# Attention values of the last 64 keys in quarters of the array, for two slots at once, and the copy of x ahead of the split

## The chip, the cores and the metric

The kernel runs on one core of a Trainium2 chip. The engines named here are TensorE (PE, with its weight loads as PEld), VectorE (DVE), ScalarE (ACT), GpSimd (POOL) and SyncE (SP, which here only issues DMAs). The metric is the device time of one execution in microseconds (us). Three runs of the kernel before gave a median of 1435.09 us, from 1433.96 to 1436.72.

## What is computed

Attention over 8 batches, 8 heads, 576 positions and a head size of 64, in which each row keeps only its 32 largest scores; then a feed-forward block with a sigmoid-gated unit. All is float32.

```python
scores = scale * np.matmul(q, k.transpose(0, 1, 3, 2))      # 576 x 576 for each batch and head
kth = np.partition(scores, -32, axis=-1)[..., -32:-31]
scores = np.where(scores >= kth, scores, -1e9)
attn = softmax(scores)
x = np.matmul(attn, v)            # (8,8,576,64), then heads side by side: 4608 rows x 512
h = x @ w_in                      # 512 x 2048
g = h / (1 + exp(-1.702 * h))
out = g @ w_out                   # 2048 x 512
```

## The kernel before

**Slots.** The work of the attention is cut into 144 slots, 18 for each batch. A slot holds 128 query rows of two heads (a pair `hp`, four pairs in a batch), so 2 x 576 scores for each of its rows. A batch has 576 = 4 x 128 + 64 rows; the last 64 rows of two pairs share one slot, so two slots of each batch are such end slots (`t == NF`), in which the two pairs take 64 columns each.

**What a slot goes through.** PE makes the scores in 64x64 quarters of its array (`scores`, L312): the contraction is over a head's 64 dimensions, one head in the upper and one in the lower half of the array's rows, and each head's scores go to banks of their own. ACT copies them out of PSUM with the scale (`copy_scores`, L324). DVE makes pairwise maxima and minima of the two halves of each row (`pair_up`, L334, two TENSOR_TENSOR), and then finds the 32 largest in four rounds of MAX8 with MATCH_REPLACE8 between them (`topk`, L348 and L352). POOL makes two small bounds (`bounds`, L366 and L367), ACT masks (L379) and takes exponentials with their sums (L387). DVE inverts the sums (`invert`, L395 and L397, the tile `rden`), POOL multiplies the probabilities by it (`normalize`, L410, two instructions), and ACT splits each float32 into its two 16-bit halves (`split`, L446). SP writes these to DRAM (L448) and reads them back transposed (`turn_by_dma`, L454) into the tile `pt`, in which keys lie on the partitions. `pt` has nine blocks of 128 keys: four whole blocks of the one head, one block made of the last 64 keys of both heads (the one head on partitions 0 to 63, the other on 64 to 127), and four whole blocks of the other head.

**Values.** `values_at` (L504) multiplies `pt` with the values `v`: for each slot five products for each head, 128 keys deep and 64 columns wide in the array, so that the two heads run side by side. The fifth product uses the tile `tail` (v_e in the profile): the 64 last keys of head j lie in the half of the partitions that belongs to head j in `pt`, and the other half of the partitions is zero, so that the product runs over all 128 partitions and drops the other head's keys. Tails are loaded by `load_v` (L218, two DMAs) into four tiles that stay. ACT copies the result out of PSUM (`x_of`, L527, L530) into `xs`, the input of the feed-forward block.

**Feed-forward.** Four slots complete a block of 128 rows of x. `hidden` (L570) makes 4 of 16 pieces of h for a block, in one bank `ph`; ACT takes the tanh (L586) and copies h (L589); POOL forms the gate (`gate`, L598 and L599) and four sums (`combine`, L623 to L626) for a product by a scheme with seven instead of eight block products; PE projects (`project`, L677). When a block is done ACT copies the two banks (L695), and POOL adds the seven products up (`merge_all`, five TENSOR_TENSOR, L702) before the output leaves.

**Order.** The order of the instructions of every engine is written out by hand. From slot 13 on it is the order of `two_slots(n)` (L1018), called for every second n. One call holds, for PE: two `hidden`, scores of n+2, two projections, the values of slots n-3 and n-2 (`held`), scores of n+3. DVE finds the largest of slot n and of n+1 (`find`, L956): 14 instructions of `topk` with `pair_up` of the next slot after the eighth (i == 7), and `invert` of the slot before after instruction `at`, which is 8. POOL: merge_all, combine, normalize(n-1), gate, bounds(n), combine, normalize(n), gate, bounds(n+1). ACT: split(n-1), copy_scores(n+2), mask and exponentials of n, tanh and h, split(n), x_of, copy_scores(n+3), mask and exponentials of n+1, tanh and h. While `filling` (up to n = 19) x_of stands right behind the values instead.

**PSUM.** Eight banks: two score tiles of two banks each, two for the projection, and two in the pool `ps_t`, which hold in turn the two `ph` and the one `o` (values) of each call. A tile of the pool waits until the tile two before it has been read.

Of the kernel before, what the change touches and what calls it, by code (L numbers as in the profile page):

```python
# [11 lines left out]
F32 = mybir.dt.float32  # L12
# [6 lines left out]
P = 128  # L19
# [11 lines left out]
def kernel(  # L31
# [27 lines left out]
    nc = tc.nc  # L59

    B, H, S, D = q.shape
# [3 lines left out]
    NF = S // P  # L65
    FULL = NF * P
    TAIL = S - FULL
# [9 lines left out]
    MAIN = (0, NF + 1)  # L77
# [29 lines left out]
    xs = const.tile([P, PLACES, CC, P], F32, name="xT")  # L107
# [5 lines left out]
    ps_t = pool("ps_t", 2, space=PSUM)  # L113
# [52 lines left out]
    qT, kT, vv = {}, {}, {}  # L166
# [41 lines left out]
    def load_v(b, hp):  # L208
        main = vals.tile([P, 2, NF, D], F32, name="v_l")
        nc.sync.dma_start(  # L210
            main[:].rearrange("p j t d -> p j (t d)"),
            v[b, 2 * hp : 2 * hp + 2, 0:FULL, :].rearrange("j (p t) d -> p j (t d)", t=NF),
        )


        tail = v_ends[(b * NP + hp) % len(v_ends)]
        for j in range(2):
            nc.sync.dma_start(tail[j * TAIL : (j + 1) * TAIL, j, :], v[b, 2 * hp + j, FULL:S, :])  # L218
        vv[b, hp] = main, tail

    def prepare_main(name, b, hp):
# [68 lines left out]
    second_part = []  # L290


    slots = []
    for b in range(B):

        full = [(b, t, (hp, hp)) for t in range(NF) for hp in range(NP)]
        ends = [(b, NF, (hp, hp + 1)) for hp in range(0, NP, 2)]
# [2 lines left out]
    PER = N // B  # L300
    st = [{} for _ in slots]

    def scores(n):
        b, t, hps = slots[n]
        ps = [ps_s.tile([P, 2, 512], F32, name="s_ps") for _ in range(2)]
        quadrants = (0, 0), (1, 1), (0, 1), (1, 0)
        of = lambda p: slice(t * P + p * TAIL, t * P + (p + 1) * TAIL) if t < NF else slice(FULL, S)
        parts = [(i, p, slice(p * TAIL, (p + 1) * TAIL), of(p)) for i, p in quadrants]
        for c in range(2):
            for i, p, rows, cols in parts:  # L310
                on = slice(i * D, (i + 1) * D)
                nc.tensor.matmul(  # L312
                    ps[i][rows, c, 0:HALF],
                    lhsT=qT[b, hps[p]][on, cols],
                    rhs=kT[b, hps[p]][on, FIRST[i] + c * HALF : FIRST[i] + (c + 1) * HALF],
                )
        st[n]["ps"] = ps
# [10 lines left out]
    def pair_up(n):  # L328

        sc = st[n]["sc"]  # L330
        a, b = sc[:, :, 0:HALF], sc[:, :, HALF:S]
        ranked[n] = rank.tile([P, 2, 2, HALF], F32, name="ranked")
        for c, op in enumerate((ALU.max, ALU.min)):
            nc.vector.tensor_tensor(out=ranked[n][:, :, c, :], in0=a, in1=b, op=op)  # L334
# [34 lines left out]
    def exponentials(n, between=lambda: None):  # L369

        mask(n)
        between()
        exps(n)
# [18 lines left out]
    def invert(n):  # L392

        some = small.tile([P, 2], F32, name="some", tag="sums")
        nc.vector.tensor_scalar_add(some[:], st[n]["den"][:], 1e-9)  # L395
        rden = st[n]["rden"] = small.tile([P, 2], F32, name="rden", tag="inverse")
        nc.vector.reciprocal(rden[:], some[:])  # L397
# [44 lines left out]
    def split(n):  # L442

        pr, sc = st[n]["pr"], st[n]["sc"]
        halves = sc[:].rearrange("p i k -> p (i k)").bitcast(U16).rearrange("p (h k) -> p h k", h=2)
        nc.scalar.copy(out=halves, in_=pr[:].bitcast(U16).rearrange("p (k h) -> p h k", h=2))  # L446
        rows = st[n]["rows"] = apart.tile([P, 2, 2 * S], U16, name="rows")
        nc.sync.dma_start(rows[:], halves)  # L448
# [10 lines left out]
    def place_of(b, t):  # L459

        name = (b, t) if t < NF else b // 2
        if name not in places:
            places[name] = free.pop(0)
        return places[name]
# [39 lines left out]
    def values_at(m, o):  # L504

        b, t, hps = slots[m]
        pt = st[m]["pt"]
        for p in range(2 if t == NF else 1):
            cols = slice(p * TAIL, (p + 1) * TAIL) if t == NF else slice(0, P)
            main, tail = vv[b, hps[p]]  # L510
            for c in range(NF + 1):
                for j in range(2):
                    nc.tensor.matmul(  # L513
                        o[j * D : (j + 1) * D, cols],
                        lhsT=main[:, j, c, :] if c < NF else tail[:, j, :],
                        rhs=pt[:, MAIN[j] + c if c < NF else NF, cols],
                        start=(c == 0),
                        stop=(c == NF),
                    )
        st[m].clear()  # L520

    def x_of(held, o):

        b, t, hps = slots[held[0]]
        x = xs[:, place_of(b, t), :, :]
        if t < NF:
            nc.scalar.copy(out=x[:, hps[0] : hps[0] + 2, :], in_=o[:, 0:2, :])  # L527
        else:
            parts = o[:, 0:2, :].rearrange("p s (h r) -> p (s h) r", h=2)
            nc.scalar.copy(out=x[:, :, b % 2 * TAIL : (b % 2 + 1) * TAIL], in_=parts)  # L530
        for m in held:
            finish_x(m)

    def finish_x(m):

        b, t, hps = slots[m]
        if hps[-1] < NP - 1:
            return
        if t == NF:
            if b % 2:  # L540
                first = [(b - 1 + i) * S + FULL for i in range(2)]
                ready.append(Block(places.pop(b // 2), [out[x : x + TAIL, :] for x in first]))
            return
        lines = out[b * S : b * S + FULL, :].rearrange("(p t) c -> p t c", t=NF)[:, t, :]
        ready.append(Block(places.pop((b, t)), [lines[i * TAIL : (i + 1) * TAIL, :] for i in range(2)]))
# [189 lines left out]
    def at(n, fn, *args):  # L735
        later.setdefault(n, []).append((fn, args))
# [36 lines left out]
    def finish_one():  # L773
        unfinished.pop(0)()
# [179 lines left out]
    live = lambda m: 0 <= m < N  # L954

    def find(m, at):  # L956

        for i, op in enumerate(topk(m) if live(m) else [lambda: None] * 14):
            op()
            if i == 7 and live(m) and live(m + 1):  # L960
                pair_up(m + 1)
            if i == at and live(m - 1):
                invert(m - 1)
            if i > 1 and len(unfinished) > (2 if m == SETTLED + 1 else 0):
                finish_one()

    def project_one():
        if may_project(0):
            project(True)
# [48 lines left out]
    def two_slots(n):  # L1018

        begin, prepare_some = dues(n)  # L1020
        aside = n < N
        filling = n < STEADY + 8
        if live(n - 1):
            exponentials(n - 1)
        if n == STEADY or n > STEADY + 4:
            prepare_some()
        hidden(ps_t)
        hidden(ps_t)
        tanh(aside)
        if live(n + 2):  # L1030
            scores(n + 2)
        project_one()
        merge_all()
        combine()
        project_one()
        find(n, 8)
        if live(n - 1):
            normalize(n - 1)
            split(n - 1)
        gate()  # L1040
        begin(0)
        if live(n - 1):
            turn_by_dma(n - 1)
        while turns:
            turns.pop(0)()
        if live(n + 2):
            copy_scores(n + 2)
        if live(n):
            bounds(n)
            mask(n)  # L1050
        combine()
        sum_weights(4)
        if live(n):
            exps(n)
        tanh(aside)
        prepare_some()
        held = [m for m in (n - 3, n - 2) if live(m)]
        o = ps_t.tile([P, 4, P], F32, name="o", tag="tp") if held else None
        ends = [(b, hp, o[:, 2 + i, :]) for i, (b, hp) in enumerate(second_part)]
        second_part.clear()  # L1060
        for what in ends:
            turn_qk_ends(*what)
        for i, m in enumerate(held):
            values_at(m, o[:, i, :])
        if filling and held:
            x_of(held, o)
        for what in ends:
            copy_qk_ends(*what)
        if filling:
            begin(1)  # L1070
        if live(n + 3):
            scores(n + 3)
        leave_all()
        find(n + 1, 8)
        if live(n):
            normalize(n)
            split(n)
        if held and not filling:
            x_of(held, o)
        if not filling:  # L1080
            begin(1)
        if live(n):
            turn_by_dma(n)
        gate()
        if live(n + 3):
            copy_scores(n + 3)
        if live(n + 1):
            bounds(n + 1)
        sum_weights(4)
# [51 lines left out]
```

## Time and profile before

| what | value |
|---|---|
| median of 3 runs | 1435.09 us |
| the profiled execution's own time | 1434.99 us |
| its span | 1433.1 us |
| mean granted TensorE clock | 0.982 |
| busy: PE, PEld | 1374.1 us (96%), 1233.0 us (86%) |
| busy: DVE | 1345.1 us (94%) |
| busy: ACT, POOL | 1165.1 us (81%), 959.3 us (67%) |
| from the values' first matmul at 291.6 us to that at 1343.5 us (58 calls of `two_slots`) | 1051.9 us; PE busy 1048.6, DVE busy 1044.4 |
| DMA share in that stretch | 0.76, granted clock 1.00 |

The chain of work that ended last gives shares of the span to the instruction that was being waited for, so it names the engine that sets the time. The timeline lists instructions by start and length in us; an instruction's successor on its engine can start before its end is recorded. "idle before, releaser" says what ended an engine's wait. A float32 matmul stands in the profile as two MATMUL instructions.

### The profile page before, as it was taken

To read this page: it belongs to the slowest core of one execution; us is meant where nothing else is said; L and a number is where in the kernel's file an instruction comes from. 1 tells how busy PE (TensorE), PEld (TensorE's weight loads), DVE (VectorE), ACT (ScalarE), POOL (GpSimd) and SP (SyncE) were. 2 spreads that over 40 slices of the span, in tenths; PEclk is the share of its full clock that TensorE was granted. 3 is DMA by queue.
4 is the path that set the end of the run, shared out by engine and by line. 5 is a ranking of instruction groups with operands and counts; after the bars stand their busy time and mean duration, and the time that the engine had idled before them with its cause. 6 is when DMAs were issued, how large, how long until landed. Compare 5 with 4: busy or idle time off the path is not lost.

```text
span 1433.1 us, 45827 instructions
## 1 busy us (share of the span) xinstructions
PE 1374.1 (96%) x18164; PEld 1233.0 (86%) x18164; DVE 1345.1 (94%) x3526; ACT 1165.1 (81%) x1895; POOL 959.3 (67%) x1602
## 2 busy tenths in 40 slices
PE   6779797899999999999999999999999999999997
PEld 5667476799999999999999999999899999999997
DVE  7999998999999999999999999999999999999712
ACT  6998777888888888888888888888888888888811
POOL 4787694677766777777777777777666677777710
PEclk8899899999999999999999999999999999999999
DMA  7452465878687788778787887887887786655520
GB/s 223 141 152 72 126 155 151 195 189 195 169 203 184 192 192 201 202 182 187 190 208 180 187 196 182 198 190 189 185 208 189 182 205 175 175 141 141 141 58 16
DMA packets 535991, 245.47 MB, mean 171 GB/s; under 512 B 458976, under 2 KB 514273, under 8 KB 535777
## 3 DMA queue, kind: packets, MB, share of 16 engines
q1 hardware_dynamic: 535344, 242.25, 68.0%
q8 instruction: 142, 2.33, 0.7%
q14 instruction: 73, 0.59, 0.1%
q10 hardware_dynamic: 432, 0.30, 0.1%
HBM read 45.09 MB, written 103.42 MB: 104 GB/s over the span
## 4 chain that ended last, share of the span: by engine, by line
PE 81%; DVE 9%; ACT 4%; POOL 2%; DMA 2%; issue 1%; SPq 0%; POOLq 0%; ACTq 0%; DVEq 0%
PE ph L570 32%; PE po L677 28%; PE o L513 10%; PE s_ps L312 9%; DVE top L348 4%; DVE ranked L352 2%; DVE left L352 1%; DVE ranked L334 1%; DMA pt<-rows 1%; ACT pr L387 1%; DMA qk_t<-qk_rows 1%; PE tp L424 1%; POOL pr L410 1%; ACT sc L379 0%; PE po L570 0%
## 5 line engine op out<-in xcount | busy, mean ns | idle before, releaser
L348 DVE MAX8 top<-ranked 128x8 f32<-128x288 f32 (+1 forms) x1080 | 598.8, 596 | 0.0
L570 PEld LDWEIGHTS ph<-xT,win 128*128 128x128 f32 x4384 | 495.2, 192 | 32.1 <-ACT sc L446 14.9
L570 PE MATMUL ph<-xT,win 128*128 128x128 f32 x4384 | 509.2, 277 | 2.5 <-ACT xT L527 2.5
L352 DVE MATCH_REPLACE8 ranked<-top,ranked 128x288 f32<-128x288 f32 (+1 forms) x810 | 433.5, 543 | 0.0
L410 POOL TENSOR_SCALAR pr<-pr,rden 128x576 f32<-128x576 f32 x268 | 197.7, 749 | 319.2 <-DVE rden L397 196.1
L446 ACT COPY sc<-pr 128x2304 uint16<-128x2304 uint16 x134 | 283.5, 2116 | 130.9 <-POOL pr L410 130.5
L334 DVE TENSOR_TENSOR ranked<-sc 128x576 f32<-128x576 f32 x270 | 218.9, 852 | 3.2 <-ACT sc L324 3.2
L387 ACT ACTIVATE pr<-sc,low 128x576 f32<-128x576 f32 x288 | 220.3, 773 | 0.0
L379 ACT ACTIVATE sc<-sc,cut 128x576 f32<-128x576 f32 x288 | 207.8, 778 | 4.6 <-POOL cut L366 4.6
L677 PE MATMUL po<-raws,h 128*64 128x128 f32 x2048 | 198.8, 273 | 0.0
L677 PE MATMUL po<-wout,h 128*64 128x128 f32 x2048 | 198.8, 273 | 0.0
L324 ACT ACTIVATE sc<-s_ps 128x576 f32<-128x576 f32 x288 | 171.7, 650 | 21.7 <-PE s_ps L312 10.8
L312 PE MATMUL s_ps<-qk_t 64*64 64x288 f32 x2304 | 177.1, 420 | 3.8 <-ACT sc L324 2.2
L599 POOL TENSOR_TENSOR th<-th,h 128x512 f32<-128x512 f32 x130 | 166.5, 1281 | 10.8
L677 PE MATMUL po<-wout,th 128*64 128x128 f32 x2176 | 168.6, 276 | 0.0
L513 PE MATMUL o<-pt,v_l 128*64 128x128 f32 (+1 forms) x2400 | 146.8, 267 | 8.1 <-DMA pt<-rows 6.7
L677 PEld LDWEIGHTS po<-wout,th 128*64 128x64 f32 x2176 | 124.3, 137 | 28.2 <-issue 20.6
L513 PEld LDWEIGHTS o<-pt,v_l 128*64 128x64 f32 x2400 | 128.5, 140 | 9.9 <-DMA pt<-rows 7.3
L677 PEld LDWEIGHTS po<-raws,h 128*64 128x64 f32 x2048 | 129.5, 137 | 0.0
L677 PEld LDWEIGHTS po<-wout,h 128*64 128x64 f32 x2048 | 129.4, 137 | 0.0
L702 POOL TENSOR_TENSOR raws<-raws 128x128 f32<-128x128 f32 (+1 forms) x165 | 93.5, 575 | 47.3 <-ACT raws L695 39.5
L312 PEld LDWEIGHTS s_ps<-qk_t 64*64 64x64 f32 x2304 | 76.1, 134 | 52.9 <-issue 14.6
(106 smaller groups left out, 1725.0 us busy)
## 6 DMA issues: line engine op xcount, KB each, us to landing
rows<-sc SPq DMA_DIRECT2D x134, 576.0 KB, 3.5
qk_rows<-halves SPq DMA_DIRECT2D x48, 256.0 KB, 3.0
out_dram<-raws SPq DMA_DIRECT2D x136, 64.0 KB, 2.3
raws<-in_moe_w_in_dram SPq DMA_DIRECT2D x16, 512.0 KB, 4.4
v_l<-in_v_dram SPq DMA_DIRECT2D x32, 256.0 KB, 3.9
raws<-in_moe_w_out_dram SPq DMA_DIRECT2D x16, 512.0 KB, 3.5
qk_l<-in_q_dram SPq DMA_DIRECT2D x60, 128.0 KB, 3.4
qk_l<-in_k_dram SPq DMA_DIRECT2D x58, 128.0 KB, 3.5
```

Source lines behind the costliest of these rows:

```text
L312: nc.tensor.matmul(ps[i][rows, c, 0:HALF], lhsT=qT[b, hps[p]][on, cols], rhs=kT[b, hps[p]][on, FIRST[i] + c * HALF : FIRST[i] + (c + 1) * ...
L324: nc.scalar.mul(out=to, in_=ps[i][:, :, 0:HALF], mul=SCALE)
L334: nc.vector.tensor_tensor(out=ranked[n][:, :, c, :], in0=a, in1=b, op=op)
L348: nc.vector.max(top[:, i, 8 * r : 8 * r + 8], of(r, i))
L352: nc.vector.match_replace(to, top[:, i, 8 * r : 8 * r + 8], of(r, i), LOWEST)
L379: nc.scalar.activation(sc[:, i, :], sc[:, i, :], AF.Prelu, bias=cut[:, i : i + 1], alpha=HUGE)
L387: nc.scalar.activation(pr[:, i * S : (i + 1) * S], sc[:, i, :], AF.Exp, bias=low[:, i : i + 1], accum_out=den[:, i : i + 1],)
L410: nc.gpsimd.tensor_scalar(pr[:, i, :], pr[:, i, :], st[n]["rden"][:, i : i + 1], 1.0, op0=ALU.mult, op1=ALU.mult)
L446: nc.scalar.copy(out=halves, in_=pr[:].bitcast(U16).rearrange("p (k h) -> p h k", h=2))
L513: nc.tensor.matmul(o[j * D : (j + 1) * D, cols], lhsT=main[:, j, c, :] if c < NF else tail[:, j, :], rhs=pt[:, MAIN[j] + c if c < NF else ...
L570: nc.tensor.matmul(ph[:, i * P : (i + 1) * P], lhsT=win[:, c, f * P : (f + 1) * P], rhs=xs[:, x.place, c, :], start=(c == 0), stop=(c == C ...
L677: nc.tensor.matmul(both_banks[y * TAIL : (y + 1) * TAIL, bank, r * P : (r + 1) * P], lhsT=a[:, i, :], rhs=weight(w, fs[i])[:, y * P : (y + ...
```

## The change

1. `load_v`: from the second batch on, each of the two DMAs of a tail brings both heads' last 64 keys (64 x 2 x 64 elements instead of 64 x 64), so both halves of the partitions hold both heads.
2. `scores`: in the slots with odd number of these batches the heads stand in opposite order (`crossed`): the head in the lower half of the array comes first in the scores and so in `pt`.
3. `values_of_two` takes the place of `values_at` for these batches: first the 16 products over whole blocks of both slots, as before; then, for the last 64 keys, four products of 64 x 64 in the four quarters of the array, two for each slot. The slot's heads in opposite order make the four quarters different ones. Each slot has a bank of its own: `o` becomes two tiles of `ps_t`.
4. `x_of`: one copy for each slot (128 x 128) instead of one for both (128 x 256), and, after the filling, in front of `split(n)` instead of behind it.
5. `find(n, 10)` and `find(n + 1, 10)` instead of 8: `invert` of the slot before stands two DVE instructions later, behind the second MAX8 and the first MATCH_REPLACE8 of the third round.

```diff
         for j in range(2):
-            nc.sync.dma_start(tail[j * TAIL : (j + 1) * TAIL, j, :], v[b, 2 * hp + j, FULL:S, :])
+            on, heads = slice(j * TAIL, (j + 1) * TAIL), slice(j, j + 1) if b == 0 else slice(0, 2)
+            src = v[b, 2 * hp + heads.start : 2 * hp + heads.stop, FULL:S, :]
+            nc.sync.dma_start(tail[on, heads, :], src.rearrange("j p d -> p j d"))
...
+    crossed = lambda n: n % 2 == 1 and slots[n][0] > 0
...
             for i, p, rows, cols in parts:
-                on = slice(i * D, (i + 1) * D)
+                j = 1 - i if crossed(n) else i
+                on = slice(j * D, (j + 1) * D)
...
+    def values_of_two(held, o):
+        order = []
+        for s, m in enumerate(held):
+            b, t, hps = slots[m]
+            pt = st[m]["pt"]
+            for p in range(2 if t == NF else 1):
+                cols = slice(p * TAIL, (p + 1) * TAIL) if t == NF else slice(0, P)
+                main, tail = vv[b, hps[p]]
+                at = lambda i: 1 - i if crossed(m) else i
+                for c in range(NF):
+                    for i in range(2):
+                        order.append((0, s, p, i, at(i), cols, main[:, at(i), c, :], pt[:, MAIN[i] + c, cols]))
+                for i in range(2):
+                    on = slice(i * TAIL, (i + 1) * TAIL)
+                    order.append((1, p, s, i, at(i), cols, tail[on, at(i), :], pt[on, NF, cols]))
+            st[m].clear()
+        bank_of = lambda x: (x[2] if x[0] else x[1], x[4])
+        order.sort(key=lambda x: x[:4] if x[0] else (0,))
+        for k, (ends, p, s, i, j, cols, lhsT, rhs) in enumerate(order):
+            if not ends:
+                p, s = s, p
+            nc.tensor.matmul(
+                o[s][j * D : (j + 1) * D, cols], lhsT=lhsT, rhs=rhs,
+                start=(s, j) not in [bank_of(x) for x in order[:k]],
+                stop=(s, j) not in [bank_of(x) for x in order[k + 1 :]],
+            )
...
     def x_of(held, o):
-        b, t, hps = slots[held[0]]
-        x = xs[:, place_of(b, t), :, :]
-        if t < NF:
-            nc.scalar.copy(out=x[:, hps[0] : hps[0] + 2, :], in_=o[:, 0:2, :])
...
+        for m, part in zip(held, o):
+            b, t, hps = slots[m]
+            x = xs[:, place_of(b, t), :, :]
+            if t < NF:
+                nc.scalar.copy(out=x[:, hps[0], :], in_=part)
...
-        find(n, 8)
+        find(n, 10)
...
-        o = ps_t.tile([P, 4, P], F32, name="o", tag="tp") if held else None
+        both = [ps_t.tile([P, 4, P], F32, name="o", tag="tp") for m in held]
+        o = [x[:, 0, :] for x in both]
...
-        for i, m in enumerate(held):
-            values_at(m, o[:, i, :])
+        if held and slots[held[0]][0] > 0:
+            values_of_two(held, o)
+        else:
+            for i, m in enumerate(held):
+                values_at(m, o[i])
...
-        find(n + 1, 8)
+        find(n + 1, 10)
         if live(n):
             normalize(n)
-            split(n)
         if held and not filling:
             x_of(held, o)
+        if live(n):
+            split(n)
```

More of the change, by code (lines that the diff above doesn't have):

```diff
@@ L520, in values_at @@
         st[m].clear()
-    def x_of(held, o):
-        b, t, hps = slots[held[0]]
-        x = xs[:, place_of(b, t), :, :]
-        if t < NF:
-            nc.scalar.copy(out=x[:, hps[0] : hps[0] + 2, :], in_=o[:, 0:2, :])
[L528 to L531, printed above, removed]
+    def values_of_two(held, o):
[20 more added lines that the diff above has]
+            nc.tensor.matmul(
+                o[s][j * D : (j + 1) * D, cols],
+                lhsT=lhsT,
+                rhs=rhs,
+                start=(s, j) not in [bank_of(x) for x in order[:k]],
+                stop=(s, j) not in [bank_of(x) for x in order[k + 1 :]],
+            )
+    def x_of(held, o):
+        for m, part in zip(held, o):
[4 more added lines that the diff above has]
+            else:
+                halves = part.rearrange("p (h r) -> p h r", h=2)
+                nc.scalar.copy(out=x[:, hps[0] : hps[0] + 2, b % 2 * TAIL : (b % 2 + 1) * TAIL], in_=halves)
             finish_x(m)
@@ L1057, in two_slots @@
         held = [m for m in (n - 3, n - 2) if live(m)]
-        o = ps_t.tile([P, 4, P], F32, name="o", tag="tp") if held else None
-        ends = [(b, hp, o[:, 2 + i, :]) for i, (b, hp) in enumerate(second_part)]
+        both = [ps_t.tile([P, 4, P], F32, name="o", tag="tp") for m in held]
+        o = [x[:, 0, :] for x in both]
+        ends = [(b, hp, both[0][:, 2 + i, :]) for i, (b, hp) in enumerate(second_part)]
         second_part.clear()
@@ L1062, in two_slots @@
             turn_qk_ends(*what)
-        for i, m in enumerate(held):
-            values_at(m, o[:, i, :])
+        if held and slots[held[0]][0] > 0:
+            values_of_two(held, o)
+        else:
+            for i, m in enumerate(held):
+                values_at(m, o[i])
         if filling and held:
```

## The prediction

> **What bounds the kernel now.** I read the page first, then the chain of waits in a steady stretch, then the timeline of one find with its POOL and ACT work. The page says that PE sets the end:
>
> ```profile
> span 1433.1 us, 45827 instructions
> ...
> PE 1374.1 (96%) x18164; PEld 1233.0 (86%) x18164; DVE 1345.1 (94%) x3526; ACT 1165.1 (81%) x1895; POOL 959.3 (67%) x1602
> ...
> PE 81%; DVE 9%; ACT 4%; POOL 2%; DMA 2%; issue 1%; SPq 0%; POOLq 0%; ACTq 0%; DVEq 0%
> ```
>
> The chain between 690 and 727 us shows one call of two_slots as PE alone, without a gap: 2.18 + 1.13 + 7.34 + 1.13 + 6.26 = 18.04 us, from values to values 18.05.
>
> ```profile
> 708.68 2.18 PE o L513 x40
> 710.86 1.13 PE s_ps L312 x16
> 711.99 7.34 PE ph L570 x64
> 719.33 1.13 PE s_ps L312 x16
> 720.46 6.26 PE po L677 x112
> ```
>
> But DVE has nothing to spare. In the 58 calls from 291.6 to 1343.5 us its waits are 3.4 us together, and its own beat is as long: from one reciprocal to the next 8.845 us in three finds of four (707.90, 716.74, 725.59 us), and 9.56 us in the fourth, so 36.10 us for four finds, 18.05 a call. PE and DVE are level. A change that shortens PE alone can win almost nothing; what it does to DVE decides.
>
> The timeline of one find, every engine but PE:
>
> ```profile
> 707.90 0.17 DVE L397 RECIPROCAL rden<-some 128x2 f32<-128x2 f32 x1
> 707.99 0.74 DVE L348 MAX8 top<-ranked 128x8 f32<-128x576 f32 x1
> 708.25 1.48 POOL L410 TENSOR_SCALAR pr<-pr,rden 128x576 f32<-128x576 f32 x2 [3.16 <-DVE rden L397]
> 708.64 0.07 DVE L352 MATCH_VALUE_LOAD ranked<-top,ranked 128x8 f32 x1
> 708.70 0.74 DVE L352 MATCH_REPLACE8 ranked<-top,ranked 128x576 f32<-128x576 f32 x1
> 709.36 0.08 DVE L352 MATCH_VALUE_LOAD ranked<-top,ranked 128x8 f32 x1
> ...
> 709.75 2.11 ACT L446 COPY sc<-pr 128x2304 uint16<-128x2304 uint16 x1 [1.84 <-POOL pr L410]
> ...
> 712.04 1.19 ACT L324 ACTIVATE sc<-s_ps 128x576 f32<-128x576 f32 x2
> ...
> 713.05 0.46 POOL L625 TENSOR_TENSOR h<-th,h 128x128 f32<-128x128 f32 x1
> 713.47 0.46 POOL L626 TENSOR_TENSOR h<-th 128x128 f32<-128x128 f32 x1
> ...
> 714.56 1.41 DVE L334 TENSOR_TENSOR ranked<-sc 128x576 f32<-128x576 f32 x2
> ```
>
> The reader is to see that POOL's and ACT's work hangs on the reciprocal (call it R): POOL waits 3.16 us for it, normalizes from R+0.35, and runs without a pause to the last sum L626, R+5.57 to R+6.0. ACT splits at R+1.85 and ends copy_scores at R+5.33. DVE's next pair_up starts at R+6.66, after both.
>
> Why one find in four takes 9.56 us is seen where POOL merges a block and is late:
>
> ```profile
> 765.76 3.03 POOL L702 TENSOR_TENSOR raws<-raws 128x256 f32<-128x256 f32 x5
> 768.34 2.00 DVE L334 TENSOR_TENSOR ranked<-sc 128x576 f32<-128x576 f32 x2
> 768.75 0.97 POOL L623 TENSOR_TENSOR h<-th 128x128 f32<-128x128 f32 x1
> ```
>
> Here pair_up meets POOL's TENSOR_TENSORs, and both slow down: 2.00 us instead of 1.41. By the starts, its first half takes 0.99 us instead of 0.67 (the merge's last addition, of 256 elements, had begun 0.28 us before it and lets go some 0.6 us after its start), the second 0.93 (one sum of 128 elements gets in between and costs 0.26). MAX8 and MATCH_REPLACE8 beside POOL keep their length. The counter-example: where the POOL sum begins with pair_up or hardly before it, DVE loses nothing and POOL waits for both halves:
>
> ```profile
> 213.18 1.75 POOL L625 TENSOR_TENSOR h<-th,h 128x128 f32<-128x128 f32 x1
> 213.20 1.41 DVE L334 TENSOR_TENSOR ranked<-sc 128x576 f32<-128x576 f32 x2
> ```
>
> The same happened with POOL ahead by 0.06 us (1321.84 against 1321.90). With POOL ahead by 0.14 us (a 512-element subtraction, at 169.6 us) POOL won, and the pair took 3.49 us.
>
> **The change part by part.**
>
> *Quarters on PE.* Before, 20 products (40 MATMULs) take 2.18 us: 0.218 for a pair side by side. Two pairs go, 0.436 us. Four quarters come; the nearest row is scores, 16 MATMULs of 64x64 with 288 columns in 1.13 us, so 8 with 128 columns are 0.565 x 128/288 = 0.25 us. Ends: 0.218 (as fast as a pair) and 0.565 (as long as the scores' eight, no better for fewer columns). I take 0.25, the same tiling by columns: 0.19 us saved, PE 17.86 us a call. Scores in 64x64 follow anyway, so no extra change of tiling. End slots alike. A rule against it, which the sum does not need: the Trainium skill, "TensorEngine Tiling (Array Packing)", section "Gotcha 1: PSUM Pressure", says that different row tiles cannot access one PSUM bank at the same time. Here the two quarters of a slot are in different row tiles and in one bank; the scores, one bank for each row half, cannot show it. By that rule the quarters would take about two pairs' time and PE stay at 18.05; by the row it is 17.86.
>
> *Tails.* 28 pairs x 2 DMAs become 64x2x64. SP's issue of that shape (L199) has a median of 0.72 us, of the old one (L218) 0.61: 0.2 us for each pair, and 16 KB more each. They are issued about a batch-slot before use; hidden, nothing. Crossing the scores moves no instruction and costs nothing.
>
> *Copy of x.* Two copies of 128x128 (0.264 each, L495) for one of 128x256 (0.374): 0.15 us more on ACT. They stand in ACT's 1.84 us of waiting for the normalize, and the split no longer has to precede the release of the bank.
>
> *Two banks.* The second slot's products now wait for the second h copy (L589 ends at 707.91; the second slot starts near 709.6), and the two next hidden for the two copies of x. Behind the waiting matmul on PE stand the quarters, scores of n+3 and both hidden; ACT's copy_scores waits for the scores. ACT's tanh and h follow the preceding split by 7.0 us, so they move with R and end near R+0.0 to R+0.4; quarters end some 1.2 us on, and x_of by R+1.9, when the split is due. No gain or loss on its own: 0, at most a few tenths, in the slack that PE has below.
>
> *invert two instructions later.* It removes one MAX8 (0.65) and a value load with MATCH_REPLACE8 (0.72) from between R and the next pair_up: this starts at R+5.28 instead of R+6.66. POOL and ACT keep their distances to R. So:
> - copy_scores ends at R+5.33-0.27 (x_of moved away) = R+5.06. It just fits: 0.
> - L625 starts at R+5.15, 0.13 us before pair_up, and lets go after about 0.33 us (0.61 less the 0.29 by which 256 elements take longer than 128, 752 against 458 ns): pair_up 0.20 us late. L626, waiting since R+5.57, gets between the halves: 0.26. Together 0.46 us a find. Ends: 0 (DVE first, as at 213.20) and 0.59 (both halves as at 768.34). I take 0.46, as 0.13 lies nearer to the 0.14 where POOL won than to the 0.06 where it lost.
> - In the find with the merge: the second addition (R+4.89) is through at R+5.2, the third begins at R+5.42 under pair_up and waits until both halves are done: DVE loses 0, but the merge and the sums then end near R+10.1, and the next normalize, due at R+9.19, starts 0.93 late.
> - In the find after it split and copy_scores are thus 0.93 late, R+6.0, and pair_up, due at R+5.28, waits about 0.8. Ends 0 (were POOL in time) and 0.93+.
>
> Four finds: 4 x 8.845 = 35.38, plus 0 + 0.8 + 0.46 + 0.46 = 37.10 us, against 36.10. DVE becomes the bound at 18.55 us a call; PE (17.86) waits and its gain vanishes.
>
> By the Trainium skill, "SBUF — State Buffer", section "Who interferes with whom", the shared port is a lock held for the whole instruction; with whole recorded lengths (0.46 us) the two delays would be 0.32 and 0.46 and two calls 37.74. The rows above show shorter holds, 0.33 and 0.26, and decide.
>
> *Sum.* 1051.9 us / 36.1 = 29.1 times 1.0 = +29. Of the 1051.9 us, 5 are not beat but PE's end slots and waits for DMA; PE's new slack takes about 3 of them. Before and after the stretch: no term, +-3 (POOL adds up weights there and pair_up already collides: 3.49 us). Profiled execution 1434.99 + 26 = 1461. It stands 0.1 us under the median of the runs, so this is also the forecast of the time.
>
> **The rivals.**
> 1. *DVE gets the port first* in the ordinary finds (threshold between 0.06 and 0.14 us ahead; I put 0.13). Then four finds are 35.38 + 0.8 = 36.18, with DVE's small "some" delayed as now (0.13) 36.3: 29 x 0.1 = +3 us, less 3 of slack: 1436. For it: only 0.07 us separates the cases.
> 2. *Faster:* the collision of the merge goes and the late normalize does not follow. Place: POOL after a merge. If normalize starts less than 0.2 us late, copy_scores is in time, DVE needs 17.7 a call, PE 17.86 decides: 58 x 0.19 = 11 us and 1 more of today's waits, 1423. It needs the port to go to DVE as well. Against it: POOL's rows leave 0.0 us of room there now (L626 ends as the next normalize begins, 771.58).
> 3. *The quarters do not overlap:* PE stays near 18.05; with rival 1, 1438, otherwise hidden under DVE.
> 4. *Worse:* both halves lose throughout (0.59 each, and 0.39 in the merge's find): 35.38 + 0.39 + 0.8 + 1.18 = 37.75, 29 x 1.65 - 3 = +45, 1480; with ACT late as well, more.
>
> **How the numbers follow.** Forecast 0.62 (its own range 1446 to 1472), rival 1 0.12, rival 2 0.15, rival 3 without the collision 0.03, rival 4 0.08. A difference under 0.2% (3 us) cannot be told from none. Faster: rival 2 and a quarter of rival 1, 0.18; same: half of rival 1 and a part of 3, 0.08; slower: the rest, 0.74. Leaving out rival 2's lower half and the upper half of rival 4 gives 1423 to 1482.
>
> **What would show it.** Right: L334 in ordinary finds near 1.87 us for its two halves (now 1.41), POOL's L625 and L626 beside it; DVE "ranked" waiting some 0.8 us for ACT copy_scores in one find of four; the beat near 18.5 us; PE with 0.7 us of waits a call at the values; the last products of o in 0.25 us. Wrong: pair_up at 1.41 us in most finds, L625 stretched to 1.7 us instead, and PE still without a gap at about 17.9 us. The forecast falls if the port goes by another order than the starts that the records show.

## The result and the profile after

The changed kernel takes 1468.98 us (median of 4 runs, 1468.36 to 1469.52) against 1435.19: a ratio of 1.0235, with a 95% interval of 1.0217 to 1.0252. It is slower by 34 us; the forecast was 1461, by 26. The profiled execution has a span of 1466.4 us. In the experiments below the kernel before takes 1431.9 us (two chips, 21 runs on each), 3 us less than here, so each of them is set against that.

The page of the changed kernel: span, busy time by engine, and the shares of the chain that ended last.

```profile
span 1466.4 us, 45956 instructions
...
PE 1372.2 (94%) x18164; PEld 1217.6 (83%) x18164; DVE 1357.6 (93%) x3526; ACT 1168.4 (80%) x1962; POOL 1022.8 (70%) x1602
...
DVE 7%; PE 5%; POOL 5%; issue 5%; ACT 4%; DMA 1%; SPq 0%; POOLq 0%; DVEq 0%; ACTq 0%
```

PE no longer carries the chain. The chain is not followed all the way here (its shares add up to a quarter), so it does not say who took PE's place; the timeline does. POOL is busy for 63 us longer with the same instructions, a sign that some of them are being held up.

First an ordinary find, the timeline of POOL, ACT and DVE from 761 us (start, length, instruction; lines are 5 later than before for DVE and ACT, 35 later for POOL's sums):

```profile
761.04 0.17 DVE L402 RECIPROCAL rden<-some 128x2 f32<-128x2 f32 x1
761.38 1.47 POOL L415 TENSOR_SCALAR pr<-pr,rden 128x576 f32<-128x576 f32 x2 [2.18 <-DVE rden L402]
762.88 2.11 ACT L451 COPY sc<-pr 128x2304 uint16<-128x2304 uint16 x1
764.90 1.18 ACT L329 ACTIVATE sc<-s_ps 128x576 f32<-128x576 f32 x2
...
766.18 0.46 POOL L660 TENSOR_TENSOR h<-th,h 128x128 f32<-128x128 f32 x1
766.30 1.87 DVE L339 TENSOR_TENSOR ranked<-sc 128x576 f32<-128x576 f32 x2
766.60 0.96 POOL L661 TENSOR_TENSOR h<-th 128x128 f32<-128x128 f32 x1
```

The reciprocal R is at 761.04. POOL and ACT are where they were behind R, and copy_scores ends at R+5.04. pair_up starts at R+5.26 instead of R+6.66, 0.12 us after POOL's third sum has begun, and takes 1.87 us instead of 1.41. POOL's fourth sum takes 0.96 us instead of 0.46, between the two halves of pair_up.

Then the find with the merge, and the one after it:

```profile
742.35 0.17 DVE L402 RECIPROCAL rden<-some 128x2 f32<-128x2 f32 x1
...
746.41 4.16 POOL L737 TENSOR_TENSOR raws<-raws 128x256 f32<-128x256 f32 x5
747.62 1.42 DVE L339 TENSOR_TENSOR ranked<-sc 128x576 f32<-128x576 f32 x2
...
751.19 0.17 DVE L402 RECIPROCAL rden<-some 128x2 f32<-128x2 f32 x1
...
752.02 0.45 POOL L661 TENSOR_TENSOR h<-th 128x128 f32<-128x128 f32 x1
752.46 1.46 POOL L415 TENSOR_SCALAR pr<-pr,rden 128x576 f32<-128x576 f32 x2
753.95 2.11 ACT L451 COPY sc<-pr 128x2304 uint16<-128x2304 uint16 x1 [2.76 <-POOL pr L415]
755.97 1.19 ACT L329 ACTIVATE sc<-s_ps 128x576 f32<-128x576 f32 x2
...
757.19 1.69 DVE L339 TENSOR_TENSOR ranked<-sc 128x576 f32<-128x576 f32 x2 [0.65 <-ACT sc L329]
757.24 1.02 POOL L660 TENSOR_TENSOR h<-th,h 128x128 f32<-128x128 f32 x1
```

Here POOL is held up instead: its five additions take 4.16 us (3.03 before), pair_up stays at 1.42. The bill comes one find later. The normalize that was due at R+0.34 starts at R+1.27, so the split starts at R+2.76 and copy_scores ends at R+5.97. DVE stands for 0.65 us and starts pair_up at R+6.00. POOL's third sum, begun 0.05 us after it, still gets in between its two halves: 1.69 us instead of 1.41.

From reciprocal to reciprocal the four finds between 742.35 and 779.63 us take 8.84, 9.85, 9.30 and 9.29 us: 37.28, where it had been 36.10. Between the values at 292.7 and at 1374.65 us, the same 58 calls as before, there are 1081.95 us, 30.0 more. The other 3.3 us of the 33.3 by which the span grew lie before (1.1) and behind (2.2).

### The profile page after: what moved, and what is told of

It is laid out like the page before. It is cut to its first block, busy times and chain, and to the rows that moved or that the text cites. A ratio compares the mean times of both kernels' runs of the same rounds, so it can differ in the third digit from the quotient of the medians.

```text
span 1466.4 us, 45956 instructions
## 1 busy us (share of the span) xinstructions
PE 1372.2 (94%) x18164; PEld 1217.6 (83%) x18164; DVE 1357.6 (93%) x3526; ACT 1168.4 (80%) x1962; POOL 1022.8 (70%) x1602
## 5 line engine op out<-in xcount | busy, mean ns | idle before, releaser
L353 DVE MAX8 top<-ranked 128x8 f32<-128x288 f32 (+1 forms) x1080 | 587.7, 595 | 0.0
L339 DVE TENSOR_TENSOR ranked<-sc 128x576 f32<-128x576 f32 x270 | 235.3, 911 | 28.8 <-ACT sc L329 28.5
L549 PE MATMUL o<-pt,v_l 128*64 128x128 f32 (+1 forms) x2240 | 135.3, 266 | 41.6 <-ACT h L624 38.0
L549 PEld LDWEIGHTS o<-pt,v_l 128*64 128x64 f32 x2240 | 114.0, 138 | 55.2 <-ACT h L624 54.1
L737 POOL TENSOR_TENSOR raws<-raws 128x128 f32<-128x128 f32 (+1 forms) x165 | 123.8, 758 | 46.5 <-ACT raws L730 38.7
L317 PEld LDWEIGHTS s_ps<-qk_t 64*64 64x64 f32 x2304 | 79.7, 135 | 44.4 <-issue 8.0
```

What stands on the lines that cost most here:

```text
L317: nc.tensor.matmul(ps[i][rows, c, 0:HALF], lhsT=qT[b, hps[p]][on, cols], rhs=kT[b, hps[p]][on, FIRST[i] + c * HALF : FIRST[i] + (c + 1) * ...
L353: nc.vector.max(top[:, i, 8 * r : 8 * r + 8], of(r, i))
L549: nc.tensor.matmul(o[s][j * D : (j + 1) * D, cols], lhsT=lhsT, rhs=rhs, start=(s, j) not in [bank_of(x) for x in order[:k]], stop=(s, j) n ...
```

## The experiments

Theory: POOL and ACT hang on the reciprocal, and `invert` two instructions later brings pair_up so near to it that POOL's sums meet pair_up in three finds of four, and ACT's copy is late in the one behind a merge. Rival: the values' second bank. In the list of waits of the changed kernel (us in total, times, longest) the longest of PE's is that of the values' weight load for ACT's release of the bank:

```profile
PEld o L549 <- ACT h L624: 54.1, 58, 8.2
```

### invert back to 8 in the changed kernel

```diff
-        find(n, 10)
+        find(n, 8)
...
-        find(n + 1, 10)
+        find(n + 1, 8)
```

> The changed kernel with invert back behind the first MAX8 of the third round (8 instead of 10); quarters, two banks and the early copy of x stay. Theory (POOL's and ACT's work hangs on the reciprocal, and pair_up now comes too soon after it): pair_up again starts 6.66 us after the reciprocal, only the find with the merge is long, four finds take 36.1 us and DVE sets 18.05 us a call, so the time is within 4 us of the kernel before, 1431 to 1437. Rival (the second bank for the values, for which PE waits 54 us in the profile of the changed kernel, is the loss): the waits stay and so does the time, 1460 or more.

Measured: 1431.71 us against 1431.91 of the kernel before on the same chip, ratio 0.9993 (0.9984 to 1.0002). The quarters, the two banks and the early copy are all still there, and the whole loss is gone. Ordinary finds are 8.84 or 8.85 us, those with the merge 9.55. This run alone does not settle the rival, since the wait for the second bank shrank along with the time: the same line of the list now reads 18.2 us, 22 times, where it read 54.1. The next run, which has no second bank, tests the rival itself. The quarters bring nothing here: DVE needs 18.05 us a call, as before.

### invert at 10 in the kernel before

```diff
-        find(n, 8)
+        find(n, 10)
...
-        find(n + 1, 8)
+        find(n + 1, 10)
```

> The kernel before with invert two instructions later (10 instead of 8) and nothing else of the change. Theory: ordinary finds 9.30 us, the one after the merge 9.85, four finds 37.3 us, so the whole loss is there without quarters or banks: 1463 to 1472. Rival (second bank and copy order): no loss, 1434 to 1437.

Measured: 1469.72 us, ratio 1.0254 (1.0239 to 1.0270). The whole loss appears with this edit alone, so it needs neither quarters nor a second bank: the rival falls here. How it is spread differs from the expectation: 104 of 110 finds between 300 and 1330 us take 9.2 to 9.3 us. The ones with a merge, expected at 8.845, take 9.2, and the ones behind them 9.3 instead of 9.85; that the total still came out as expected is in part luck. With x_of still behind the split, copy_scores ends later in every second find, and pair_up then starts at R+5.36 and not at R+5.27 (765.64 + 1.20 = 766.84 here, pair_up at 766.87). The timeline:

```profile
761.51 0.17 DVE L397 RECIPROCAL rden<-some 128x2 f32<-128x2 f32 x1
765.38 0.37 ACT L527 COPY xT<-o 128x256 f32<-128x256 f32 x1
...
765.64 1.20 ACT L324 ACTIVATE sc<-s_ps 128x576 f32<-128x576 f32 x2
...
766.65 0.46 POOL L625 TENSOR_TENSOR h<-th,h 128x128 f32<-128x128 f32 x1
766.87 1.78 DVE L334 TENSOR_TENSOR ranked<-sc 128x576 f32<-128x576 f32 x2
767.06 0.98 POOL L626 TENSOR_TENSOR h<-th 128x128 f32<-128x128 f32 x1
```

### Two of POOL's four sums less

```diff
-        engine.tensor_tensor(out=s4, in0=a12, in1=s2, op=ALU.subtract)
-        engine.tensor_tensor(out=s3, in0=a11, in1=a21, op=ALU.subtract)
+        if not aside:
+            engine.tensor_tensor(out=s4, in0=a12, in1=s2, op=ALU.subtract)
+            engine.tensor_tensor(out=s3, in0=a11, in1=a21, op=ALU.subtract)
```

> The changed kernel, invert at 10, without the last two of the four sums that POOL makes for the projection (L625 and L626 of before; the two operands keep h instead, so this part of the computation is left out). No other engine has less to do. Theory: nothing of POOL meets pair_up at 5.27 us behind the reciprocal, the merge ends before the next normalize is due, four finds are near 35.4 us, and PE's 17.86 us a call is the bound: about 45 us less than the changed kernel, 1420 to 1430. Rival (second bank or the copies): no change, 1460 or more.

Measured: 1424.3 us, ratio 0.9944 (0.9929 to 0.9959). That is 45 us less than the changed kernel took, of which some 3 us are not the edit's: the kernel before was faster by as much in these runs. The time is saved though POOL was no bound of it (70% busy) and DVE and PE have the same number of instructions. Ordinary finds are 8.84 us with invert at 10 and copy_scores ending at R+5.05: so both sums, and not the copies, make the 9.30. The chain is PE's again (77%), and the median from values to values is 17.83 us. Not as expected is the find with the merge, mostly 9.1 to 9.3 us. In the one from 615.75 us (9.16) an addition of the merge gets in between the halves of pair_up, which takes 1.69 us: 0.27 of the 0.31 us too much. The rest is a pair_up that starts at R+5.31, since the split now stands behind the copies of x, which wait for PE. This price of the early copy is mostly below 0.15 us a merge; in the find from 722.91 us, with the split at R+2.58, DVE waits 0.48 us for it.

### invert at 9 in the changed kernel

The edit is as in the first experiment, with 9.

> The changed kernel with invert one instruction later than before (9). Theory: pair_up starts 6.00 us after the reciprocal. POOL's last sum begins at 5.57 and lets go at 5.90, so ordinary finds are 8.845 us; in the find with the merge the fourth addition begins at 5.96, only 0.04 us ahead of pair_up, where POOL has lost so far, so DVE loses nothing; the merge then ends late and the next find waits about 0.2 us. Four finds 35.6 us, 17.8 a call; PE with its quarters needs 17.86 and is the bound: 1051.9 - 58 x 0.19 = 11 to 12 us less than the kernel before, 1420 to 1427. Rival (second bank): 1460 or more. If POOL wins the merge's find, 1430 to 1434.

Measured: 1432.31 us, ratio 1.0000 (0.9991 to 1.0009). The time missed the expectation by 5 us, for three reasons. The merge's find mostly went as foreseen: an addition that began 0.06 us ahead of pair_up (R+5.94 against R+6.00) had to wait. But in 5 of 29 rounds of four finds it began 0.06 to 0.13 us ahead and won, and the find took 9.7 us. In the find after the merge's, pair_up's second half also meets a sum: mostly 9.2 to 9.3 us where 9.04 was expected. And in 11 of the 29 rounds one more find is long. In that one ACT's `halves` copy of 2.11 us makes the tanh late, POOL's gate waits for it, and the sums come half a microsecond later, into pair_up:

```profile
789.67 2.11 ACT L266 COPY halves<-qk_l 128x2304 uint16<-128x2304 uint16 x1
790.06 0.17 DVE L402 RECIPROCAL rden<-some 128x2 f32<-128x2 f32 x1
...
791.67 0.61 ACT L621 ACTIVATE th<-ph 128x512 f32<-128x512 f32 x1
792.37 0.62 POOL L633 TENSOR_SCALAR th<-th 128x512 f32<-128x512 f32 x1 [0.50 <-ACT th L621]
...
796.05 1.69 DVE L339 TENSOR_TENSOR ranked<-sc 128x576 f32<-128x576 f32 x2
796.14 0.98 POOL L661 TENSOR_TENSOR h<-th 128x128 f32<-128x128 f32 x1
```

Four such finds (from 763.04 us: 8.90, 9.27, 8.84, 9.11) make 36.1 us, as much as before.

### Merge behind the sums, invert at 8

What keeps DVE at 18.05 us in the kernel before is the merge alone. If it is put behind the sums, most of it comes while pair_up is already running. The edit goes with that of the first experiment (8 instead of 10):

```diff
         project_one()
-        merge_all()
         combine()
+        merge_all()
         project_one()
```

> The changed kernel with invert at 8 and POOL's merge behind the four sums instead of ahead of them. Theory: the sums end 6.0 us after the reciprocal, the merge's first addition begins at 6.03 and lets go by 6.63, just before pair_up (6.65); the rest is held up until pair_up is done, the next normalize starts some 0.9 us late, and the sums then meet pair_up for about 0.15 us. Four finds 35.5 us instead of 36.1, DVE 17.77 us a call, so PE with its quarters (17.83 in the profiles of the last runs) becomes the bound: 58 x 0.21 = 12 us less than the kernel before, 1417 to 1424. Rival (something else than the shared port keeps DVE at 18.05): 1429 to 1434. If the first addition is in the way of pair_up, about 0.8 us a merge stays and nothing is won.

Measured: 1424.13 us, ratio 0.9951 (0.9938 to 0.9964). This is faster than both kernels, by 7.8 us than the one before (7.0 by the ratio); 4 us less gain than the middle of the expectation, whose top (1424) it just misses. pair_up is whole beside the merge:

```profile
764.97 0.46 POOL L661 TENSOR_TENSOR h<-th 128x128 f32<-128x128 f32 x1
765.38 4.17 POOL L737 TENSOR_TENSOR raws<-raws 128x256 f32<-128x256 f32 x5
766.07 1.41 DVE L339 TENSOR_TENSOR ranked<-sc 128x576 f32<-128x576 f32 x2
```

and PE runs without a gap in the chain, 17.83 us a call (here up to the next values):

```profile
759.54 2.13 PE o L549 x39
761.67 0.97 PE s_ps L317 x16
762.64 7.34 PE ph L605 x64
769.98 1.13 PE s_ps L317 x16
771.11 6.26 PE po L712 x112
```

The quarters are in the first two lines: values and the scores behind them take 3.10 us instead of 3.31. The 58 calls take 1042.4 us, 8.3 more than 58 x 17.83. Some calls are longer (398.75 us follows 379.61 by 19.1), which I have not traced one by one.

### The same exchange in the kernel before

```diff
         project_one()
-        merge_all()
         combine()
+        merge_all()
         project_one()
```

> The kernel before with the same exchange of merge and sums, without quarters, banks or early copy. Theory: DVE gets to 17.77 us a call as in the run with the quarters, but PE still needs 18.05: no more than 2 us less than the kernel before, 1429 to 1433. The difference to the run with the quarters is what the quarters are worth once DVE does not set the time: 9 to 12 us. Rival (the gain of the other run is DVE's alone): the same time as that run, 1417 to 1424.

Measured: 1431.6 us, ratio 1.0001 (0.9992 to 1.0010). Without the quarters the free DVE is worth nothing: values follow values after 18.05 us, and PE carries 80% of the chain. That DVE is free shows in its waits between 291 and 1340 us, 12.7 us for ACT's exponentials (3.1 in the kernel before). Against the run before, the quarters with their banks and the early copy are worth 7.5 us (1431.6 - 1424.13), less than the 9 to 12 expected.

### The copy of x behind the split again

```diff
-        if held and not filling:
-            x_of(held, o)
         if live(n):
             split(n)
+        if held and not filling:
+            x_of(held, o)
```

This edit is made in the fastest kernel, the one with the merge behind the sums and invert at 8.

> As the first of these runs, but the two copies of x stand behind the split again. The next hidden products then wait for a bank until about 4.2 us after the reciprocal. Theory: PE settles at a phase that fits (its whole program is 17.83 us a call and nothing in the loop is longer), copy_scores ends at 5.6 us, before pair_up at 6.65: the same time as the first of these runs within 3 us. Rival (the early copy is needed since the two banks are held longer): PE waits 1 us or more a call, 1440 and above.

Measured: 1432.81 us, ratio 1.0004 (0.9995 to 1.0013). Neither expectation holds: 8.7 us are lost, more than 3 and far from a microsecond a call. The early copy is a needed part of the gain. In the profile the weight loads of hidden wait 32.3 us for the copies between 291 and 1340 us, where the fastest kernel has 22.8. PE itself stands 6.6 us for them (5.7 for L563, 0.9 for L566), where the fastest kernel has 0.4, and about every second call takes 18.05 us instead of 17.83. copy_scores waits 18.3 us for the DMA `rows`, 4.9 in the fastest kernel:

```profile
PEld ph L605 <- ACT xT L563: 32.3, 52, 2.0
...
ACT sc L329 <- DMA rows<-sc: 18.3, 21, 2.5
...
PE ph L605 <- ACT xT L563: 5.7, 18, 1.5
```

How these make up the 8.7 us was not separated; the 58 calls take 1047.3 us, 4.9 more than in the fastest kernel, so a part of the loss also lies outside of them.

## Why the prediction was right, point by point

**PE and DVE level, so that DVE decides.** Right. With DVE held at 18.05 us the quarters bring nothing (invert at 8: ratio 0.9993), with DVE freed they bring 7.5 us.

**Quarters, 0.25 us for four.** Right within 0.02: the first of them and the first score behind them are 0.27 us apart (762.03 and 762.30 us). The saving a call is 0.22 us in the chain (18.05 to 17.83) instead of 0.19, still hidden in the changed kernel. By the starts in the kernel with the merge behind the sums, the products give 0.16 of it (from the first one to the first score 2.12 us instead of 2.28), and 0.05, for which the sum had no term, comes from the scores behind them (1.08 us to the first hidden instead of 1.13).

**Two banks and copies, tails: nothing.** Right for the changed kernel: the loss is there without the second bank (invert at 10 in the kernel before) and gone with it (invert at 8), so the waits for it are PE's spare time. SP's issue of a tail has a median of 0.65 us (0.61 before). What the text did not see is that the early copy has a worth of its own once PE is the bound: 8.7 us in the last experiment.

**invert later, pair_up at R+5.28.** Right: R+5.27. The collision with the sums was put at 0.46 us a find, 0.20 and 0.26; measured 9.30 less 8.845, with halves of about 0.87 and 0.93 us instead of 0.67 and 0.67. POOL won, being 0.13 us ahead.

**The merge's find, 0.** Right: 8.84. The normalize 0.93 us late: right, R+1.27.

**The find behind it, 0.8 us.** This term was too small: it measured 1.0. The wait for copy_scores is 0.73 (pair_up at R+6.00 instead of R+5.27), and the step left out that a sum gets in between the two halves there too, 0.27. That gives 37.28 instead of 37.10 us for four finds, and 29 x 0.18 = 5 us, which more than covers the 4 by which the forecast was short in the stretch (30.0 us instead of 29 - 3 = 26). The rest of the 8 us that were missing is the 3.3 us outside of the stretch, for which it had no term and had allowed 3.

**The rivals.** That DVE gets the port first was excluded in ordinary finds by the length of L339 (1.87 us), and holds in the merge's find. The faster case needed the normalize in time and the port with DVE; neither came with invert at 10. Its PE beat came with invert at 8 and the merge moved (17.83 us), its gain only in part (7.8 us instead of 12). The first rival's own sum does not hold together: 36.3 less 36.1 us is 0.2 a round and not 0.1, which gives 29 x 0.2 - 3 = 3 us and 1438, not 1436. Nothing hangs on it.

## What to carry to other kernels

When two engines are level, ask first what the change does to the one that it does not mean to help: here a small operation moved by 1.4 us cost 34 us, because everything on two other engines is timed from it. Look for the instructions of two engines that slow each other, and measure their distance to the instruction that both follow; a busy share does not show it. When a shortened engine brings nothing, find what holds the other one, and move that (here the merge) before giving the idea up.

## What the runs showed of the hardware

- Who gets in first between a POOL TENSOR_TENSOR and DVE's two-input TENSOR_TENSOR goes by the starts within about 0.1 us where DVE comes to it without a wait: POOL ahead by 0.13 us wins (changed kernel); with invert at 9, POOL ahead by 0.04 to 0.05 us loses, at 0.06 us it loses and wins, and at 0.09 us it wins. Where DVE had just waited 0.65 us for ACT, POOL won though it was only 0.04 us ahead (invert at 10 in the kernel before, pair_up at 599.32 us: 2.23 us).
- When DVE comes first, two things are seen, both in the changed kernel. At 747.62 us POOL waits for both halves of pair_up (the third addition of the merge starts at R+5.41 and ends at R+7.00). At 757.19 us POOL's sum waits for the first half only and gets in between the two, for 0.26 us. DVE had waited for ACT in the second case and not in the first, but at 796.05 us with invert at 9 a sum gets in between without such a wait, so what decides stays open. When POOL comes first, its next sum gets in between the halves as well (766.60 us).
- Four products of 64x64 of one set start within 0.02 us of each other (762.030 to 762.050 us) though the two of a slot use different halves of the array's rows and one bank. The Trainium skill, "TensorEngine Tiling (Array Packing)", section "Gotcha 1: PSUM Pressure", rules out simultaneous access of different row tiles to one bank; with different partitions in the bank these runs show no delay by it.
